# A written order for VectorE and ScalarE in the attention loop of a fused attention and mixture-of-experts kernel

## The chip, the cores and the metric

The kernel runs on one core of one Trainium2 chip. The time is device microseconds of one execution. Before the change it is 614.98 us, the median of three runs (613.36 to 615.66 us). The profile is that of one more execution, which took 612.03 us; what the profiler recorded of it spans 610.3 us.

The engines are named as in the profile: PE is the matrix engine (PEld its weight loads), DVE the vector engine, ACT the scalar engine, POOL the general engine, SP the engine that issues most transfers. A program holds one list of instructions for each engine; which of two instructions that could both run stands first in such a list is decided when the program is built, and that is the subject of this change.

## What is computed

The reference is sliding-window attention with sinks (4 batches, 8 heads, 768 positions, head size 64, window 128, the first 4 positions kept for everyone), and behind it a mixture of 8 experts in which a token may stay with the expert of the token before it:

```python
scores = scale * q @ k.T                      # per batch and head
keep = is_sink | ((rel >= 0) & (rel < window))
a = softmax(where(keep, scores, -1e9))
x = (a @ v)                                   # -> (B, S, 512)
logits = x @ w_gate;  local = sigmoid(x @ w_local)
for s in range(S):                            # per batch, in order
    e = argmax(logits[s]) if s == 0 or local[s] < 0.5 else e_of(s - 1)
    out[s] = softmax(logits[s])[e] * (relu(x[s] @ w1[e]) @ w2[e])
```

The choice of an expert needs the whole row of attention outputs of a token (all 8 heads), and it runs through the positions of a batch in order.

## The kernel before

**Attention.** The work is cut into 8 groups (`gi` 0 to 7: 4 batches times 2 halves of 4 heads), each into 6 blocks of 128 queries (`i` 0 to 5), each into two units of 2 heads (`c` 0 and 1; `k = 2 i + c` numbers the units of a group). A block sees its own 128 keys, the 128 before them and 8 sink columns, so a row of scores has 264 columns (128 in block 0, 256 in block 1). Float32 products are made exact enough by splitting queries and keys into a high and a low part: the high part is a cast by DVE or ACT (line 124), the low part a subtraction by POOL or DVE (line 129).

The loop (line 738) is a software pipeline over blocks. One turn of it, called here **the turn of block n**, does:

- `score` for both units of block n: 12 matmuls (line 539), then for each of the 4 heads an eviction on DVE, which adds the mask and finds the row's bound (line 543), and an exponential on ACT (line 546);
- `slot`: what belongs to other groups: loads, the split of the next group's queries and keys in four steps (`head`, at the units that `HEADS` names), in the last group the split of the first expert weights (`first_split`);
- `turn` of block n-1, unit 0: 4 transposes into PSUM (line 561) and a copy out by ACT (line 563);
- `apply` of block n-2, unit 1: 8 matmuls with the values (line 596), one for the sinks (line 602), and `finish`, four DVE instructions (lines 511 to 517);
- `turn` of block n-1, unit 1: the same, and for the sinks a transpose of a small tile (line 568), matmuls that prepare columns of the next group's values in the same PSUM bank (line 493), a copy by ACT (line 573), a subtraction by DVE (line 577) and a copy by DVE (line 464); behind the last block of a group three more DVE instructions (lines 474 to 479, `sink_rows`);
- `apply` of block n-1, unit 0; and one `step` of the routing.

The transposes and the sink tile share two PSUM buffers (`ps_t`). Three tiles go through them in a turn, so the sink transpose (line 568) takes the buffer that ACT's first copy of the turn (line 563) has to empty.

**Routing** of a batch begins two turns behind its last block, in the turn of block 1 of groups 2, 4 and 6, and goes on by one part per turn (two per turn in the last group): two reductions; eight small DVE instructions; a transpose of flags with copies by ACT; a scan over 768 positions (line 285); a second scan (line 289) with a product on POOL, or on DVE for the last batches (line 292); in block 0 of the next group a matmul (line 297) and seven small DVE instructions; then the scatter of the rows (line 312). The last batch is routed in two pieces, the first of them in the last turns of attention.

**What sets the order.** PE follows the program text (`manual_schedule(engines={ET.PE})`, line 727). DVE, ACT, POOL and SP are put in order by a planner that goes by its own estimate of when inputs are ready; `issue_after` gives it single constraints (for example, a split of the next group not ahead of the unit's last eviction and exponential). Behind attention, in the expert part, all engines but POOL follow the text.

**The start.** `lead0` splits the first 256 columns of group 0, `rest0` the others; the first two of `lead0`'s four steps stand ahead of the loop, the other two behind the first unit's scores. `products` and `logits` prepare group 0's own value columns, `rest` its sink rows.

Of the kernel before, what the change touches and what calls it, by code (L numbers as in the profile page):

```python
# [68 lines left out]
def kernel(ctx, tc, qkd, vn, vtd, vs, w1, w2, nw, c_misc, c_ident, c_small,  # L69
# [345 lines left out]
    def attention(fast):  # L415
        sfx = "f" if fast else "g"
        with ExitStack() as st:
# [17 lines left out]
            def group_steps(b, g, res):  # L435
# [17 lines left out]
                def products(j):  # L453
                    if j in ((0, 2) if fast else (0,)):
                        t["m"], t["j"] = ps_m.tile([P, NBLK * HG + 2 * WIDE, NW], F32, tag=m_tag, name=f"vw{n}_{j}"), j
                    for pr in range(npr):
                        o = ((j - t["j"]) * npr + pr) * 2
                        nc.tensor.matmul(t["m"][:, o:o + 2 * WIDE, :], vt_t[:, pr, j * P:(j + 1) * P],
                                         wb[:, g * npr + pr:g * npr + pr + WIDE, :], start=True, stop=True)

# [66 lines left out]
            def score(u):  # L527
# [13 lines left out]
                for t in range(2):  # L541
                    sm = p3.tile([P, N2], F32, tag="sm", bufs=4, name=f"sm{n}_{t}")
                    u["dve"] = nc.vector.tensor_tensor_reduce(out=sm[:, :w], in0=sps[:, t, :w], in1=mk, scale=-0.125,  # L543
                                                   scalar=BIG, op0=ALU.add, op1=ALU.min,
                                                   accum_out=bias[:, t:t + 1])
                    u["act"] = nc.scalar.activation(pe[:, t, :w], sm[:, :w], AF.Exp, bias=bias[:, t:t + 1], scale=-1.0)  # L546

                if c == 1 and i >= 2:
                    u["blk"]["pk"] = pk = p2.tile([P, 3, HG, SK], F32, tag="pk", name=f"pk{n}")
                    nc.vector.tensor_copy(  # L550
                        pk, u["blk"]["pe"][:, :, P:P + SK].unsqueeze(1).broadcast_to([P, 3, HG, SK]))

            def turn(u):
# [5 lines left out]
                for t in range(2):  # L559
                    for k, (j, o) in enumerate(tiles):  # L560
                        u["after"] = [nc.tensor.transpose(tp[:, t, k, :], pe[:, t, o:o + P], ident)]  # L561
                u["pt"] = pt = p3.tile([P, 2, 2, P], F32, tag="pt", name=f"pt{n}")
                u["after"].append(nc.scalar.copy(pt[:, :, 0:nt, :], tp[:, :, 0:nt, :]))  # L563
                if c == 1 and i >= 2:
                    nr, r0, r1 = 3 * HG * SK, HG * SK, 2 * HG * SK
                    both = ps_t.tile([P, 512], F32, tag="t", name=f"tps{n}")
                    tps = both[0:nr, 0:P]
                    nc.tensor.transpose(tps, u["blk"]["pk"].rearrange("p a h s -> p (a h s)"), ident)
                    if u["ahead"]:
                        vw = both[:, P:P + 2 * (HG + WIDE - 1) * NW].rearrange("p (x c) -> p x c", c=NW)  # L570
                        mm, out = u["ahead"]["spare"](vw, i)
                    u["blk"]["pts"] = pts = p2.tile([nr, P], F32R, tag="pts", name=f"pts{n}")
                    hi = nc.scalar.copy(pts, tps)
                    if u["ahead"]:
                        tc.add_manual_dep(hi.ins, mm.ins.name, mybir.DependencyInfo(
                            mybir.DependencyClass.Sync, mybir.DependencyReason.DATA), reason="one bank")
                    lo = nc.vector.tensor_tensor(out=pts[r0:r1], in0=tps[r0:r1], in1=pts.bitcast(F32)[r0:r1],  # L577
                                                 op=ALU.subtract)
                    u["after"].append(lo)
                    if u["ahead"]:  # L580
                        with tc.issue_after(lo.ins):
                            out()
# [83 lines left out]
            if fast:  # L666
# [12 lines left out]
                def slot(u, gi, k):  # L679
# [8 lines left out]
                    if gi == 0:  # L688
                        with tc.issue_after(units[k]["dve"].ins), tc.issue_after(units[k]["act"].ins):
                            for f in rest0[2 * k - 2:2 * k] if 0 < k < 3 else []:  # L690
                                f()
                        if k == RK:
                            with tc.issue_after(units[RK]["dve"].ins):
                                gst[0]["rest"]()
                        for x in LOADS.get(k, ()):
                            qk_load(x) if x > 1 else gst[nx]["load"][x]()
                        if k < 3:
                            gst[0]["products"](2 * k)
                            gst[0]["products"](2 * k + 1)
                        if k == 0:  # L700
                            gst[0]["logits"](0, 2)
# [25 lines left out]
                order.enter_context(tc.manual_schedule(engines={ET.PE}))  # L727

                def drain(u):
                    with ExitStack() as late:  # L730
                        for x in u["after"]:
# [543 lines left out]
```

## Time and profile before

| | |
|---|---|
| median of 3 runs | 614.98 us |
| profiled execution | 612.03 us |
| its span | 610.3 us |
| attention, until PE starts on the experts | 252.6 us |
| expert part | 357.7 us |
| PE busy in the span | 554.3 us (91%) |
| DVE, ACT, POOL busy | 373.5, 276.1, 209.9 us |

A row of the timeline has the start in us, the length in us, the engine, the line, the operation, output and inputs, the number of equal instructions merged in it, and in brackets how long the engine stood idle before it and what ended that. A row of the view by stretches has the stretch, its length, and for each engine the busy time and, in brackets, the number of instructions; then the clock granted to PE (1.00 is full), the share of the DMA engines and their rate. A row of the waits has the engine and line that waited, the engine and line that ended the wait, the us in total, the times, and the longest.

### The profile page before, as it was taken

How to read it: one execution, taken by the hardware profiler on the slowest of the kernel's cores; microseconds unless marked ns; L12 is line 12 of the kernel's file. 1: busy time of each engine (PE TensorE's matmuls, PEld its weight loads, DVE VectorE, ACT ScalarE, POOL GpSimd, SP SyncE). 2: the span in 40 equal slices, each digit the busy share in tenths (PEclk: the TensorE clock that was granted, in tenths of full speed). 3: DMA queues.
4: the chain of work that ended last, by engine and by line, in shares of the span. 5: the costliest groups of instructions: out<-in, count | busy, mean ns of one | idle time of the engine just before them, and what ended most of it. 6: DMA issues, size and time to landing. Idle time of an engine off the chain costs nothing. (4 is left out here: it accounts for less than half of the span.)

```text
span 610.3 us, 11598 instructions
## 1 busy us (share of the span) xinstructions
PE 554.3 (91%) x3872; PEld 485.6 (80%) x3872; DVE 373.5 (61%) x1268; ACT 276.1 (45%) x666; POOL 209.9 (34%) x147
## 2 busy tenths in 40 slices
PE   6799989998998879779789999989899799999995
PEld 4688978897997778667769978887887769888894
DVE  4667688778868988474637527464365767372421
ACT  2566675757566646232316218161532536132220
POOL 3233143714552750131516206253340355302201
PEclk8999999999999989789579999999999999999998
DMA  8645424643643232128438026484642629211000
GB/s 309 242 173 176 132 106 137 212 171 98 200 148 127 103 126 84 59 75 307 145 96 301 37 74 258 132 279 127 225 157 63 248 80 338 80 38 38 35 21 34
DMA packets 31481, 88.38 MB, mean 145 GB/s; under 512 B 3886, under 2 KB 5422, under 8 KB 31280
## 3 DMA queue, kind: packets, MB, share of 16 engines
q1 hardware_dynamic: 26528, 73.29, 35.8%
q0 software_dynamic: 4176, 12.64, 5.6%
q14 instruction: 147, 1.20, 0.7%
q8 instruction: 54, 0.88, 0.6%
q10 hardware_dynamic: 576, 0.36, 0.2%
HBM read 71.27 MB, written 16.06 MB: 143 GB/s over the span
## 5 line engine op out<-in xcount | busy, mean ns | idle before, releaser
L546 ACT ACTIVATE pef<-smf,biasf 128x264 f32<-128x264 f32 (+2 forms) x192 | 85.2, 488 | 79.2 <-DVE biasf L543 67.5
L596 PE MATMUL avf<-v,ptf 128*128 128x128 f32 (+1 forms) x704 | 96.9, 279 | 2.6 <-ACT ptf L563 2.2
L596 PEld LDWEIGHTS avf<-v,ptf 128*128 128x128 f32 x704 | 87.0, 193 | 5.4 <-ACT ptf L563 5.4
L543 DVE CUSTOM_DVE_ANT_0 smf<-sf,mask 128x264 f32<-128x264 f32 (+2 forms) x192 | 68.4, 403 | 16.1 <-PE sf L539 14.9
L978 ACT ACTIVATE hx<-h 128x256 fp32r<-128x256 f32 (+3 forms) x72 | 24.2, 360 | 109.2 <-PE h L967 94.4
L1016 PE MATMUL late<-w_a,hx 128*128 128x512 f32 (+2 forms) x288 | 68.8, 393 | 1.0 <-issue 1.0
L946 DVE SCALAR_TENSOR_TENSOR hx<-h,hx 128x256 fp32r<-128x256 f32 (+3 forms) x72 | 26.6, 390 | 67.7 <-ACT hx L978 66.1
L1016 PEld LDWEIGHTS late<-w_a,hx 128*128 128x128 f32 (+2 forms) x288 | 50.7, 179 | 14.4 <-issue 1.4
L1016 PE MATMUL late<-w_b,hx 128*128 128x512 f32 (+1 forms) x216 | 55.5, 414 | 2.8 <-SPq L891 2.3
L129 POOL TENSOR_TENSOR qk_b<-raw,qk_b 128x800 fp32r<-128x800 f32 (+1 forms) x16 | 31.1, 1942 | 77.1 <-PE avf L596 31.0
L561 PE MATMUL tpf<-ident,pef 128*128 128x128 f32 x352 | 56.9, 280 | 0.3 <-DVE ptsf L577 0.2
L998 POOL DMA_INDIRECT out_dram<-ot_d,oi_d x18 | 18.7, 1041 | 99.9 <-DVE ot_d L997 80.6
L1016 PEld LDWEIGHTS late<-w_b,hx 128*128 128x128 f32 (+1 forms) x216 | 41.9, 197 | 13.9 <-issue 2.5
L563 ACT COPY ptf<-tpf 128x512 f32<-128x512 f32 (+1 forms) x96 | 51.3, 535 | 3.4 <-PE tpf L561 3.1
L978 ACT ACTIVATE hx<-hs 128x96 fp32r<-128x96 f32 (+2 forms) x72 | 16.7, 273 | 70.7 <-DVE hs L961 63.7
L561 PEld LDWEIGHTS tpf<-ident,pef 128*128 128x128 f32 x352 | 39.4, 141 | 6.9 <-DVE ptsf L577 0.3
L847 POOL TENSOR_TENSOR w_b<-raw,w_b 128x1024 fp32r<-128x1024 f32 x10 | 25.6, 2558 | 39.7 <-ACT w_b L846 38.0
L847 POOL TENSOR_TENSOR w_c<-raw,w_c 128x1024 fp32r<-128x1024 f32 x11 | 27.3, 2486 | 33.5 <-ACT w_c L846 22.2
L847 POOL TENSOR_TENSOR w_a<-raw,w_a 128x1024 fp32r<-128x1024 f32 x10 | 26.5, 2649 | 30.1 <-ACT w_a L846 27.0
L967 PEld LDWEIGHTS h<-x_a,w_c 128*128 128x128 f32 x288 | 33.9, 188 | 1.7 <-issue 1.6
L129 POOL TENSOR_TENSOR w_a<-raw,w_a 128x800 fp32r<-128x800 f32 (+3 forms) x16 | 26.5, 1665 | 24.7 <-PE avf L596 13.3
L967 PE MATMUL h<-x_a,w_c 128*128 128x256 f32 x288 | 34.3, 279 | 0.8 <-DMA out_dram<-ot_d,oi_d 0.5
(239 smaller groups left out, 1063.7 us busy)
## 6 DMA issues: line engine op xcount, KB each, us to landing
raw<-in_dram SPq DMA_DIRECT2D x53, 512.0 KB, 6.1
raw<-in_dram SPq DMA_DIRECT2D x14, 800.0 KB, 4.4
vt<-in_dram SPq DMA_DIRECT2D x8, 864.0 KB, 4.7
v<-in_dram SPq DMA_DIRECT2D x7, 888.0 KB, 4.9
xr_0n<-xs SPq DMA_DIRECT2D x21, 258.0 KB, 4.1
raw_w<-in_dram SPq DMA_DIRECT2D x7, 512.0 KB, 5.8
raw<-in_dram SPq DMA_DIRECT2D x10, 256.0 KB, 3.0
xs<-zrun SPq DMA_DIRECT2D x9, 258.0 KB, 5.4
```

What stands on the lines that cost most here:

```text
L129: lows[e] = getattr(nc, e).tensor_tensor(out=out, in0=raw, in1=hi.bitcast(F32), op=ALU.subtract)
L543: u["dve"] = nc.vector.tensor_tensor_reduce(out=sm[:, :w], in0=sps[:, t, :w], in1=mk, scale=-0.125, scalar=BIG, op0=ALU.add, op1=ALU.min, ...
L546: u["act"] = nc.scalar.activation(pe[:, t, :w], sm[:, :w], AF.Exp, bias=bias[:, t:t + 1], scale=-1.0)
L561: u["after"] = [nc.tensor.transpose(tp[:, t, k, :], pe[:, t, o:o + P], ident)]
L563: u["after"].append(nc.scalar.copy(pt[:, :, 0:nt, :], tp[:, :, 0:nt, :]))
L596: nc.tensor.matmul(av[:, h, 0:w], u["pt"][:, t, k, :], u["prep"]["vf"][:, vo:vo + w], start=h == 0 and k == 0, stop=h == HG - 1 and k == l ...
L847: todo += [lambda s=s: lo(out=l[:, s], in0=raw[:, s], in1=h.bitcast(F32)[:, s], op=ALU.subtract) for s in ([slice(0, FF)] if eng[1] == "po ...
L946: nc.vector.scalar_tensor_tensor(out=d[:, :, 1, :], in0=h, scalar=0.0, in1=d.bitcast(F32)[:, :, 0, :], op0=ALU.max, op1=ALU.subtract)
L967: nc.tensor.matmul(hs, w[:, k, fs], x, start=t == 0, stop=t == len(mm) - 1)
L978: relu = nc.scalar.activation(d[:, :, 0, :], h, AF.Relu)
L998: s_i = nc.gpsimd.indirect_dma_start(out=out, out_offset=bass.IndirectOffsetOnAxis(ap=oi[0:m].bitcast(U32), axis=0), in_=ot[0:m], in_offse ...
L1016: nc.tensor.matmul(o, a, w, start=t == 0, stop=t == len(mm) - 1, skip_group_check=half)
```

## The change

DVE and ACT follow the program text in the attention loop, as PE does, and the text is rearranged for it. In a turn DVE now has: the four evictions; `finish`; the spread of the sink columns (line 550 before); the subtraction and copies behind the sink transpose; the DVE parts of `slot`; the DVE parts of the routing `step`. ACT has: the exponentials of unit 0; the copy of the first transposes; the exponentials of unit 1; the copy of the second transposes; the sink copy; the ACT parts of `slot`; those of the `step`. POOL and SP are still ordered by the planner.

Besides: the steps of the split move (`HEADS`), from units 4, 6, 8, 9 to 0, 4, 6, 8 in groups 1 to 6, and from 6, 7, 9, 10 to 4, 5, 7, 9 in group 0. All of `lead0` stands ahead of the loop, and all of `rest0` is in the turn of block 0, with one low part moved from DVE to POOL (`SENG2`). Group 0's products stand between the scores of its first two units, its `sink_mm` ahead of the copy out of the same bank. In the drain behind the last block, the transposes of the first experts' rows (`x_steps`) stand among the last turns, and the routing parts are no longer all in front of the last transposes.

```diff
-HEADS = (6, 7, 9, 10), (4, 6, 8, 9)
+HEADS = (4, 5, 7, 9), (0, 4, 6, 8)
+SENG2 = ("vector", "gpsimd", "act", "vector"), ("vector", "gpsimd", "act", "gpsimd")
...
-    rest0 = qk_split(0, SENG, False, slice(lead, S), slice(lead, KPAD))[0]
+    rest0 = qk_split(0, SENG2, False, slice(lead, S), slice(lead, KPAD))[0]
...
-        for f in lead0[0:2]:
+        for f in lead0:
...
                 def rest():
-                    logits(2, NBLK)
                     m2 = t["m"][0:nr, NBLK * HG, :]
                     sink_mm(m2)
+                    logits(2, NBLK)
                     sink_rows(m2)
...
-                    u["act"] = nc.scalar.activation(pe[:, t, :w], sm[:, :w], AF.Exp, bias=bias[:, t:t + 1], scale=-1.0)
...
+                def evict():
+                    for t in range(2):
...
+                def exps():
+                    for t in range(2):
...
+                def spread():
+                    if i >= 2:
...
+                return evict, exps, spread
...
+            def turn_sinks(u):
...
+                def rests():
+                    nc.vector.tensor_tensor(out=pts[r0:r1], in0=tps[r0:r1], in1=pts.bitcast(F32)[r0:r1],
+                                            op=ALU.subtract)
                     if u["ahead"]:
...
+                        out()
+
+                return rests
...
-                            for f in rest0[2 * k - 2:2 * k] if 0 < k < 3 else []:
-                                f()
+                        for f in rest0[2 * k:2 * k + 2]:
+                            f()
...
-                        with tc.issue_after(u["dve"].ins), tc.issue_after(u["act"].ins):
-                            head(nx, when.index(k))
+                        head(nx, when.index(k))
...
-                order.enter_context(tc.manual_schedule(engines={ET.PE}))
+                order.enter_context(tc.manual_schedule(engines={ET.PE, ET.DVE, ET.Activation}))
...
-                        score(u)
-                        for f in lead0[2:] if n + u["c"] == 0 else []:
-                            f()
-                    for u in now:
-                        slot(u, u["gi"], u["k"])
+                        parts.append(score(u))
+                        if n + u["c"] == 0:
+                            vw01 = [gst[0]["products"](j) for j in range(4)][0]
+                    for evict, _, _ in parts:
+                        evict()
+                    if now:
+                        parts[0][1]()
                     if a[0]:
                         turn(a[0])
+                    if now:
+                        parts[1][1]()
+                    if n == nu:
+                        xs_steps = [x_steps(xr0[j], early_x, j, f"{sfx}e{j}", ps_s, "s") for j in range(NE)]
                     if n >= 2 * NPR:
+                        if n > nu:
+                            while pend:
+                                step()
                         apply(z[1])
                         done(z[1]["b"], z[1]["g"], z[1]["i"])
+                    rests = None
                     if n == nu:
-                        drain(z[1])
+                        xs_steps[0][0]()
                     if a[1]:
                         turn(a[1])
+                        rests = turn_sinks(a[1])
+                    if n == nu:
+                        xs_steps[1][0]()
+                    if now:
+                        parts[1][2]()
+                    if rests:
+                        rests()
+                    if a[1]:
                         apply(a[0])
+                    if n == nu:
+                        for j in range(NE):
+                            xs_steps[j][1]()
+                    for u in now:
+                        slot(u, u["gi"], u["k"], vw01)
                     for _ in range(1 if n < nu - ST2 else 2):
-                        with tc.issue_after(now[-1]["dve"].ins) if now else ExitStack():
-                            step()
+                        step()
```

More of the change, by code (lines that the diff above doesn't have):

```diff
@@ L459, in products @@
                                          wb[:, g * npr + pr:g * npr + pr + WIDE, :], start=True, stop=True)
+                    return t["m"]
                 def logits(j0, j1, m=None):
@@ L560, in turn @@
                     for k, (j, o) in enumerate(tiles):
-                        u["after"] = [nc.tensor.transpose(tp[:, t, k, :], pe[:, t, o:o + P], ident)]
+                        nc.tensor.transpose(tp[:, t, k, :], pe[:, t, o:o + P], ident)
                 u["pt"] = pt = p3.tile([P, 2, 2, P], F32, tag="pt", name=f"pt{n}")
[L563 to L568, printed above, removed]
-                    if u["ahead"]:
[L570 to L582, printed above, removed]
@@ new lines, in turn @@
+                nc.scalar.copy(pt[:, :, 0:nt, :], tp[:, :, 0:nt, :])
+            def turn_sinks(u):
+                b, g, i, c = u["b"], u["g"], u["i"], u["c"]
+                n = f"{sfx}{b}_{g}_{i}_{c}"
+                if i < 2:
+                    return lambda: None
+                nr, r0, r1 = 3 * HG * SK, HG * SK, 2 * HG * SK
+                both = ps_t.tile([P, 512], F32, tag="t", name=f"tps{n}")
+                tps = both[0:nr, 0:P]
+                nc.tensor.transpose(tps, u["blk"]["pk"].rearrange("p a h s -> p (a h s)"), ident)
+                if u["ahead"]:
+                    vw = both[:, P:P + 2 * (HG + WIDE - 1) * NW].rearrange("p (x c) -> p x c", c=NW)
+                    mm, out = u["ahead"]["spare"](vw, i)
+                u["blk"]["pts"] = pts = p2.tile([nr, P], F32R, tag="pts", name=f"pts{n}")
+                hi = nc.scalar.copy(pts, tps)
+                if u["ahead"]:
+                    tc.add_manual_dep(hi.ins, mm.ins.name, mybir.DependencyInfo(
+                        mybir.DependencyClass.Sync, mybir.DependencyReason.DATA), reason="one bank")
+                def rests():
+                    nc.vector.tensor_tensor(out=pts[r0:r1], in0=tps[r0:r1], in1=pts.bitcast(F32)[r0:r1],
+                                            op=ALU.subtract)
+                    if u["ahead"]:
+                        out()
+                return rests
@@ L677, in head, with slot @@
                     preps[gi]["steps"][h]()
-                def slot(u, gi, k):
+                def slot(u, gi, k, vw01=None):
                     nx = gi + 1
@@ L726, in attention @@
                 order = ExitStack()
-                order.enter_context(tc.manual_schedule(engines={ET.PE}))
-                def drain(u):
-                    with ExitStack() as late:
-                        for x in u["after"]:
-                            late.enter_context(tc.issue_after(x.ins))
-                        while pend:
-                            step()
-                        for _ in early_prep(sfx, ps_s, "s"):
-                            pass
+                order.enter_context(tc.manual_schedule(engines={ET.PE, ET.DVE, ET.Activation}))
                 for n in range(0, nu + 2 * NPR, NPR):
-                    now = units[n:n + NPR]
+                    now, parts = units[n:n + NPR], []
+                    a, z = units[n - NPR:n] if 0 < n <= nu else [None, None], units[n - 2 * NPR:n - NPR]
                     for u in now:
@@ L743, in attention @@
                         if u["gi"] == 0 and u["k"] == 6:
-                            with tc.issue_after(units[5]["act"].ins), tc.issue_after(lows["gpsimd"].ins):
+                            with tc.issue_after(lows["gpsimd"].ins):
                                 xb_meta(0)
```

35 lines of the change are left out of this document (16 added, 19 removed).

## The prediction

> **What bounds the kernel now.** I read the view by stretches first, cut at the first score matmul of a group, then PE's waits. A routing group (the first row, group 2), a plain one (group 3), the last group, and from its last block to the experts:
>
> ```profile
> 67.67:96.99 29.32, 26.57 (x247) 23.84 (x246) 24.51 (x101) 19.36 (x45) 8.69 (x5) 1.00 0.36 124
> 96.99:123.89 26.90, 26.15 (x247) 24.18 (x246) 19.76 (x99) 17.63 (x42) 14.78 (x13) 1.00 0.60 192
> 210.10:236.41 26.31, 22.04 (x189) 19.92 (x189) 21.62 (x95) 14.06 (x37) 13.81 (x11) 0.94 0.35 123
> 236.41:252.62 16.21, 10.28 (x89) 9.26 (x88) 11.13 (x49) 6.29 (x16) 2.88 (x3) 0.97 0.15 53
> ...
> PE tpsf L568 <- ACT ptf L563: 10.4, 12, 1.8
> PE avf L602 <- DVE ptsf L577: 2.7, 1, 2.7
> PE avf L596 <- ACT ptf L563: 2.2, 6, 1.0
> PE tmf L297 <- DVE orr L292: 2.1, 1, 2.1
> ```
>
> PE sets the pace: in the plain group it idles 26.90 - 26.15 = 0.75 us, in a routing group 2.75, in the last 4.3. What it waits for is mostly ACT's first copy of a turn (10.4 us in 12 waits of the sink transpose). So the change can gain a few us at most in each group; where DVE or ACT come later than now, it loses.
>
> A turn without a stall, that of block 5 of group 1:
>
> ```profile
> 62.78 1.01 PE L539 MATMUL sf<-qk_b 64*128 64x264 f32 x12
> 63.49 0.43 DVE L543 CUSTOM_DVE_ANT_0 smf<-sf,mask 128x264 f32<-128x264 f32 x1 [0.22 <-PE sf L539]
> 64.02 0.92 ACT L546 ACTIVATE pef<-smf,biasf 128x264 f32<-128x264 f32 x2 [1.33 <-DVE biasf L543]
> 64.85 0.56 ACT L563 COPY ptf<-tpf 128x512 f32<-128x512 f32 x1
> 65.68 0.27 PE L568 MATMUL tpsf<-ident,pkf 128*96 128x128 f32 x1
> 66.88 0.26 ACT L573 CAST ptsf<-tpsf 96x128 fp32r<-96x128 f32 x1 [0.17 <-PE tpsf L493]
> 67.49 0.23 DVE L464 COPY v<-tpsf 128x72 f32<-128x72 f32 x1
> 67.67 0.89 PE L539 MATMUL sf<-w_a 64*128 64x128 f32 x12
> ```
>
> Here ACT already has the order that the change writes down: two exponentials, copy, two exponentials, copy. Let e be how far into a turn the first eviction starts; here 63.49 - 62.78 = 0.71. The copy starts 1.36 behind it and ends at 65.41, 0.27 ahead of the sink transpose (2.90 into the turn). DVE's last copy ends at 67.72, 0.05 into the next turn, and the next eviction could start 0.71 into it. **So 0.66 us of DVE work fit behind the copies; what is longer makes the next e late.**
>
> **The routing turns** show what a late e costs:
>
> ```profile
> 134.30 1.89 POOL L129 TENSOR_TENSOR qk_b<-raw,qk_b 128x800 fp32r<-128x800 f32 x1 [14.12 <-PE avf L596]
> 134.90 1.32 DVE L264 SCALAR_TENSOR_TENSOR frf<-lgf,small 128x6 f32<-128x6 f32 x1
> ...
> 140.15 0.31 PE L568 MATMUL tpsf<-ident,pkf 128*96 128x128 f32 x1 [1.77 <-ACT ptf L563]
> ...
> 144.75 3.00 DVE L285 TENSOR_TENSOR_SCAN orr<-kpf,fof 8x768 fp32r<-8x768 bf16 x1
> ...
> 149.22 0.43 DVE L543 CUSTOM_DVE_ANT_0 smf<-sf,mask 128x264 f32<-128x264 f32 x1
> 150.64 1.80 DVE L289 TENSOR_TENSOR_SCAN ctf<-ones,zrun,orr 8x768 f32<-8x768 f32 x1
> 151.20 0.31 PE L568 MATMUL tpsf<-ident,pkf 128*96 128x128 f32 x1 [0.74 <-ACT ptf L563]
> ...
> 237.06 0.15 DVE L264 SCALAR_TENSOR_TENSOR frf<-lgf,small 128x3 f32<-128x3 f32 x1
> ```
>
> The planner put the scan behind the evictions, and the next first eviction came late (149.22); the sink transpose followed it by 151.20 - 149.22 = 1.98. So **PE's stall is e + 1.98 - 2.90 = e - 0.92**. And line 264 took 1.32 beside POOL's low part, ending at 136.22 with it (136.19), against 0.15 alone: POOL holds such instructions up until it is done.
>
> **The change, part by part.** Unstalled turns (blocks 3 to 5 of plain groups) stay: the cast fits the 0.66, ACT's cast of queries lies behind its sink copy, long before the next exponential. A queries step also issues a load on SP; it moves at most two turns forward, its data are wanted a group later: nothing.
>
> *Key cast in block 0* (groups 1, 2, 4, 6). It stands behind the sink rows and ahead of the evictions of block 1:
>
> ```profile
> 184.82 0.98 PE L539 MATMUL sf<-w_a 64*128 64x256 f32 x12
> 185.34 0.46 DVE L479 TENSOR_TENSOR srf<-sxf,srf 32x296 fp32r<-32x296 f32 x1
> 185.83 0.42 DVE L543 CUSTOM_DVE_ANT_0 smf<-sf,mask 128x256 f32<-128x256 f32 x1
> 187.57 0.71 PE L596 MATMUL avf<-v,ptf 128*128 128x128 f32 x4 [0.15 <-ACT ptf L563]
> 189.82 0.57 DVE L124 CAST qk_b<-raw 128x800 fp32r<-128x800 f32 x1
> ```
>
> The sink rows end 0.98 into the turn, e is 1.01 and PE already waits 0.15 (stall e - 0.86). The cast adds its 0.57 in full: 4 x 0.57 = +2.3. Behind it on DVE are the evictions, for them ACT waits, for ACT PE. A gain is excluded: DVE has no gap there.
>
> *Stalls of plain groups.* Casts between evictions or ahead of a copy go:
>
> ```profile
> 112.53 0.31 PE L568 MATMUL tpsf<-ident,pkf 128*96 128x128 f32 x1 [0.47 <-ACT ptf L563]
> 131.97 0.97 DVE L247 TENSOR_REDUCE lgf<-lw 128x54 f32<-128x432 f32 x1
> 217.03 1.07 DVE L303 TENSOR_SCALAR smf<-smf 128x6 f32<-128x6 f32 x1
> ```
>
> 0.47 here, and some 0.15 of line 596's 2.2 us in 6 waits: -0.6 in groups 1, 3, 5, -1.8 (0 to -2.3, the whole 0.75 of idling).
>
> *Routing groups 2, 4, 6.* Now 1.77 + 0.74 and a small one, 2.7 of the 2.75. In the new order each part stands at the end of DVE's list, straight ahead of the evictions. Block 2: `finish` ends with the turn before it, the reduction (0.97, with its second 1.2) comes behind, e = 1.2, stall 0.4 by block 1's rule. Block 3: eight small instructions, 0.15 to 0.2 each, 1.3 in all, e = 1.4, stall 0.5. Block 4: ACT's copies of the flags ahead of its exponentials, 0.4 as an estimate from 0 to the 0.74. Block 5: the scan, 1.80 like the second one if unheld (3.00 beside POOL): e = 0.05 + 0.1 + 1.8 = 2.0, stall 1.1. Sum 2.4, so -0.3 each, **-0.9**; if POOL holds block 3's instructions for a low part (1.89), +1.7 each, +4.2.
>
> *Blocks 0 and 1 of groups 3 and 5.* Block 0: the second scan (1.80) gives e = 1.9; its evictions are half as long, so I take 0.8. Block 1: behind the sink rows (0.6 into the turn, PE being late too) come the cast (0.57) and the seven small instructions behind line 297's matmuls (1.2): e = 2.4, stall 1.6. But the cast starts POOL's low part, 1.89 long, and line 303 was held beside POOL work (1.07): then e = 0.6 + 0.57 + 1.9 + 0.9 = 4.0, stall 3.1. The held rows are the nearest, so 0.8 + 3.1 = 3.9 twice: **+7.8** (unheld +4.8).
>
> *Start.*
>
> ```profile
> 15.68 1.19 PE L539 MATMUL sf<-w_a 64*128 64x256 f32 x12
> 16.55 0.42 DVE L543 CUSTOM_DVE_ANT_0 smf<-sf,mask 128x256 f32<-128x256 f32 x1 [1.50 <-PE sf L539]
> 19.92 0.51 PE L468 MATMUL vwf<-misc,vt 128*96 128x9 f32 x4 [1.97 <-DVE v L464]
> 21.80 1.00 PE L539 MATMUL sf<-w_a 64*128 64x264 f32 x12
> ```
>
> Sink matmuls ahead of the copy remove 1.97. PE's first turn ends earlier, but DVE now has all of `rest0` in front of block 1's evictions, which stay at about 16.6. Taken -1.5 (0, if `rest0` comes later still, to -3.4, the 1.97 with 1.4 of the earlier scores).
>
> *Last group.*
>
> ```profile
> 217.56 0.45 PE L568 MATMUL tpsf<-ident,pkf 128*96 128x128 f32 x1 [1.30 <-ACT ptf L563]
> 219.21 1.96 PE L596 MATMUL avf<-v,ptf 128*128 128x128 f32 x8
> 224.78 1.00 PE L539 MATMUL sf<-qk_b 64*128 64x264 f32 x12
> 249.92 0.18 DVE L517 TENSOR_TENSOR lw<-avf,rsf 128x36 f32<-128x36 f32 x1
> ```
>
> In blocks 0 and 1 PE lost 2.7 (line 602), 1.30, and about 1.7 by matmuls at twice their length (8 in 1.96): 5.7. Weight splits no longer stand among these scans. New: scan and product, 2.8 in all, e = 2.9, stall 1.7; then 15 small instructions, e = 3.0, stall 2.1: 3.8, so -1.9 (-3.9 to 0). Tail, 236.41 to 250.10: the wait for line 297 (2.1) stays, since its two scans still run in the last turns, now with only the last `apply` behind it; transposes of the experts' rows fill about 1 of it, while splits and two routing parts make block 5's evictions about 2 late: +1.0 (-2.1 to +4).
>
> Sum: 2.3 - 1.8 - 0.9 + 7.8 - 1.5 - 1.9 + 1.0 = **+5.0**. The profiled execution took 612.03 us, so 617.0; the median of the runs is 614.98, 2.95 above it, so 620.0 for a median.
>
> The clock: line 596's 8 matmuls took 1.96 at 219.21, behind two gaps of 2.67 and 1.30. The Trainium skill (TensorE: Matmul & The Clock Gate, The HAM clock gate) wants an idle window of some 3.4 us before the clock halves; by that page stalls of 3.1 cost no clock, and the sum stays. The row shows the slowing with work between the gaps, so it speaks for the second rival below; no run here yet shows a gap of 3.1.
>
> **The rivals.**
> 1. *The wanted gain.* DVE catches up inside the turn: the casts and routing parts, ready at once, run while PE is in `apply`, so the terms for the key cast and for groups 3 and 5 are nil. For: DVE is busy only 24.51 of 29.32 us. Against: its order is one list, and the parts stand where 0.66 is free. It decides for the gain if evictions in routing turns start below e = 0.92. Then -1.8 - 0.9 - 1.5 - 1.9 + 1.0 = -5.1: 609.9.
> 2. *Clock and holds on top.* Each stall of 3.1, and the tail's, halves the clock for as long as 219 shows (1.7): three times 1.7 = +5.1, 625.1; with holds in block 3 (+1.7 three times) 630.
> 3. *Stalls only change place.* POOL starts later, nothing is held (-3.0), and the start gains 3.4 (-1.9): +0.1, 615.1. That the planner's order was already the written one speaks for it in plain turns only.
>
> **Chances.** Forecast 0.42 (own range 617 to 623), rival 1 0.22, rival 2 0.16, rival 3 0.20. No change means within 0.5%, 3.1 us. Slower: 0.42 + 0.16 = 0.58; same 0.20; faster 0.22. The range 609 to 626 leaves out the lower half of rival 1 and the holds of rival 2, some 0.18.
>
> **What would show it.** First evictions of block 1 in groups 3 and 5 at e near 4 with line 596 waiting about 3; in groups 2, 4, 6 at 1.6 with 0.7; line 568 waiting in blocks 2 to 5 for 0.4 to 1.1 instead of 1.77; line 468 no longer waiting at 20 us. Line 596 waiting under 1 in groups 3 and 5 would make the prediction wrong.

## The result: 617.11 us after 613.81 us, and the profile after

The changed kernel took 617.11 us (median; 613.58 to 623.62), the kernel before 613.81 us beside it (609.63 to 618.86): the ratio is 1.0057, with a 95% interval of 1.0033 to 1.008. It is slower, by about 3.3 us.

The profiled execution of the changed kernel took 620.67 us, 3.6 above its own median, that of the kernel before 612.03, 1.8 below its. The traces therefore differ by 8.6 us where the medians differ by 3.3. The changed kernel was profiled a second time on another chip (run *after_again* below: 616.14 us beside 614.13, a difference that is not clear of the noise); what both profiles show is the change, what only one shows is that execution.

The view by stretches of the changed kernel, cut at the first score matmul of a group as in the prediction (columns: from:to, length, busy time of PE, weight loads, DVE, ACT and POOL, granted clock, DMA share, GB/s):

```profile
68.15:96.99 28.84, 26.62 (x247) 23.84 (x247) 22.17 (x101) 19.43 (x45) 8.82 (x4) 1.00 0.34 115
96.99:126.42 29.43, 26.41 (x247) 24.20 (x246) 22.03 (x99) 17.60 (x42) 15.81 (x13) 1.00 0.52 184
...
213.55:238.62 25.07, 21.72 (x189) 19.83 (x189) 18.97 (x89) 13.98 (x35) 10.91 (x10) 0.93 0.38 136
238.62:259.28 20.66, 12.86 (x89) 11.69 (x88) 15.60 (x52) 7.61 (x19) 5.64 (x5) 0.79 0.10 33
```

The same view of the second execution, group 3 and the last stretch:

```profile
95.53:126.08 30.55, 27.78 (x248) 25.53 (x248) 22.13 (x99) 17.70 (x42) 15.46 (x13) 0.94 0.51 177
...
238.27:258.04 19.77, 11.93 (x88) 10.90 (x88) 15.58 (x52) 7.50 (x19) 5.46 (x5) 0.88 0.10 31
```

| stretch (us) | before | after | again | after - before | predicted |
|---|---|---|---|---|---|
| start, to block 2 of group 0 | 21.80 | 22.17 | 20.61 | +0.37 / -1.19 | -1.5 |
| rest of group 0 | 19.25 | 19.55 | 19.67 | +0.30 | 0 |
| group 1 (plain) | 26.62 | 26.43 | 26.44 | -0.19 | 0 |
| group 2 (routing; 4 is alike) | 29.32 | 28.84 | 28.81 | -0.48 | +0.3 |
| group 3 (plain) | 26.90 | 29.43 | 30.55 | +2.53 / +3.65 | +3.3 |
| group 5 (plain) | 26.90 | 29.43 | 29.42 | +2.53 | +3.3 |
| group 6 (routing) | 29.97 | 28.79 | 28.82 | -1.18 | +0.3 |
| group 7, blocks 0 to 4 | 26.31 | 25.07 | 25.05 | -1.24 | -1.9 |
| last block to the experts | 16.21 | 20.66 | 19.77 | +4.45 / +3.56 | +1.0 |
| experts | 357.68 | 359.12 | 356.96 | +1.44 / -0.72 | 0 |

Groups 3 and 5 and the last stretch lose; groups 1, 2, 4, 6 and 7 gain a little; the start and the experts differ in sign between the two executions. PE's waits of the changed kernel between 20 and 262 us (total, times, longest), against the 10.4, 2.7, 2.2 and 2.1 us that the prediction shows:

```profile
PE avf L615 <- ACT ptf L575: 11.8, 14, 2.1
PE tpsf L585 <- ACT ptf L575: 9.7, 11, 3.1
PE tmf L298 <- DVE orr L293: 2.7, 1, 2.7
```

PE still waits for ACT's copy of transposes, but now it is `apply` (line 615) as much as the sink transpose (line 585). Block 1 of group 3, in order of time, shows the chain:

```profile
103.53 0.58 DVE L125 CAST w_a<-raw 128x800 fp32r<-128x800 f32 x1
104.32 0.17 DVE L304 TENSOR_SCALAR smf<-smf 128x6 f32<-128x6 f32 x1
104.34 1.89 POOL L130 TENSOR_TENSOR w_a<-raw,w_a 128x800 fp32r<-128x800 f32 x1 [3.50 <-DVE smf L303]
105.07 1.19 DVE L310 TENSOR_TENSOR xb<-ppf,smf 128x6 f32<-128x6 f32 x1
106.18 0.41 DVE L548 CUSTOM_DVE_ANT_0 smf<-sf,mask 128x256 f32<-128x256 f32 x1
106.69 0.91 ACT L554 ACTIVATE pef<-smf,biasf 128x256 f32<-128x256 f32 x2 [4.79 <-DVE biasf L548]
107.50 0.35 ACT L575 COPY ptf<-tpf 128x256 f32<-128x256 f32 x1
107.91 0.71 PE L615 MATMUL avf<-v,ptf 128*128 128x128 f32 x4 [2.12 <-ACT ptf L575]
```

The key cast and seven routing instructions stand ahead of the evictions; the last of them (line 310) is held until POOL's low part is done, at 106.23. ACT has been idle for 4.79 us: its next two instructions are exponentials, and the copy that `apply` needs stands behind them. The last group's block 5 has the same chain, and there PE waits 3.13 us:

```profile
240.36 0.47 DVE L257 TENSOR_TENSOR eqf<-lgf,mxf 128x24 f32<-128x24 f32 x1
240.87 1.20 DVE L258 TENSOR_TENSOR eqf<-eqf,small 128x24 f32<-128x24 f32 x1
242.83 0.43 DVE L548 CUSTOM_DVE_ANT_0 smf<-sf,mask 128x264 f32<-128x264 f32 x1
...
244.81 0.45 PE L585 MATMUL tpsf<-ident,pkf 128*96 128x128 f32 x1 [3.13 <-ACT ptf L575]
245.05 1.92 PE L615 MATMUL avf<-v,ptf 128*128 128x128 f32 x8
```

The last row is the clock: eight matmuls in 1.92 us at a granted clock of 0.5, where the same eight took 1.06 us one turn earlier (the stretch has 0.79 on the mean). The rows by stretches divide the loss of this stretch. PE is busy for 12.86 us where it was 10.28, and idle for 7.80 where it was 5.93; in the second execution it is 11.93 and 7.84. So 1.9 us of the loss are idle time in both, and 2.6 or 1.7 us are the same matmuls at half clock.

### The profile page after: what moved, and what is told of

Its sections match the earlier page's. It is cut to its first block, busy times and chain, and to the rows that moved or that the text cites. A ratio compares the mean times of both kernels' runs of the same rounds, so it can differ in the third digit from the quotient of the medians.

```text
span 618.4 us, 11603 instructions
## 1 busy us (share of the span) xinstructions
PE 556.9 (90%) x3872; PEld 489.1 (79%) x3872; DVE 370.2 (60%) x1267; ACT 276.1 (45%) x666; POOL 211.1 (34%) x148
## 5 line engine op out<-in xcount | busy, mean ns | idle before, releaser
L615 PE MATMUL avf<-v,ptf 128*128 128x128 f32 (+1 forms) x704 | 99.5, 284 | 11.8 <-ACT ptf L575 11.8
L615 PEld LDWEIGHTS avf<-v,ptf 128*128 128x128 f32 x704 | 89.5, 198 | 15.1 <-ACT ptf L575 15.1
L548 DVE CUSTOM_DVE_ANT_0 smf<-sf,mask 128x264 f32<-128x264 f32 (+2 forms) x192 | 66.6, 401 | 14.4 <-PE sf L541 13.8
L573 PE MATMUL tpf<-ident,pef 128*128 128x128 f32 x352 | 58.7, 287 | 4.1 <-DMA xs<-zrun 3.5
L130 POOL TENSOR_TENSOR qk_b<-raw,qk_b 128x800 fp32r<-128x800 f32 (+1 forms) x16 | 33.8, 2116 | 74.4 <-ACT qk_b L125 27.6
L130 POOL TENSOR_TENSOR w_a<-raw,w_a 128x800 fp32r<-128x800 f32 (+4 forms) x17 | 28.2, 1659 | 35.3 <-ACT w_a L125 9.5
```

Of the source, the lines that this page charges most:

```text
L130: lows[e] = getattr(nc, e).tensor_tensor(out=out, in0=raw, in1=hi.bitcast(F32), op=ALU.subtract)
L548: u["dve"] = nc.vector.tensor_tensor_reduce(out=sms[t][:, :w], in0=sps[:, t, :w], in1=mk, scale=-0.125, scalar=BIG, op0=ALU.add, op1=ALU.m ...
L615: nc.tensor.matmul(av[:, h, 0:w], u["pt"][:, t, k, :], u["prep"]["vf"][:, vo:vo + w], start=h == 0 and k == 0, stop=h == HG - 1 and k == l ...
```

## The experiments

Three theories stood at the start. **T** is the prediction's: DVE work that stands straight ahead of the evictions sets the time. **U**: the loop is neutral, the loss is in the last group and the tail. **V**: the clock adds to each long stall. The runs were made on three chips: *heads_old*, *heads_mid*, *step_mid* and *fsk2* on one, where the kernel before took 625.25 us; *after_again*, *pe_only*, *pe_act* and *step_fin* on a second (614.13); the last four on a third (625.13). Ratios are each to the kernel before on the same chip.

**The splits back in the old blocks** (*heads_old*).

```diff
-HEADS = (4, 5, 7, 9), (0, 4, 6, 8)
+HEADS = (6, 7, 9, 10), (4, 6, 8, 9)
```

> The fixed order stays, only the splits go back to the blocks of the kernel before (key casts at the end of blocks 2 and 4 in groups 1 to 6, none in block 0). Theory T (DVE work that stands straight ahead of the evictions sets the time): the 0.58 us cast leaves the way to block 1, so the stalls of 0.63 to 0.64 us in block 1 of groups 1, 2, 4 and 6 fall to 0.1 (-2.2 us), the 2.12 us ones of groups 3 and 5 fall to 0.5 (-3.2 us), and blocks 3 and 5 get 0.2 to 0.6 us each back where a cast and a routing part now share a turn's end (+2 us): about -3.5 us against the changed kernel, ratio to the kernel before 1.000. Theory U (the loop is neutral, the loss is in the last group and the tail): within 0.5 us of the changed kernel, ratio 1.006.

Measured: 638.77 us, ratio 1.0215 [1.0175, 1.0255]: far slower than the changed kernel, where T expected a gain. T's first half holds: block 1 of groups 1, 2, 4 and 6 stalls 0.15 us, of groups 3 and 5 0.75. The price of its second half, +2 us, was far too low, for two reasons, shown by group 2 (POOL and DVE, then the waits, then stretches of 3.4 us):

```profile
82.81 1.89 POOL L130 TENSOR_TENSOR qk_b<-raw,qk_b 128x800 fp32r<-128x800 f32 x1 [13.50 <-issue]
82.83 1.94 DVE L258 TENSOR_TENSOR eqf<-eqf,small 128x48 f32<-128x48 f32 x1
96.41 3.37 DVE L286 TENSOR_TENSOR_SCAN orr<-kpf,fof 8x768 fp32r<-8x768 bf16 x1
...
87.47 0.31 PE L585 MATMUL tpsf<-ident,pkf 128*96 128x128 f32 x1 [2.33 <-ACT ptf L575]
101.65 0.32 PE L585 MATMUL tpsf<-ident,pkf 128*96 128x128 f32 x1 [2.75 <-ACT ptf L575]
...
85.10:88.50 3.40, 1.06 (x10) 1.03 (x10) 2.86 (x16) 2.47 (x6) 0.00 (x0) 1.00 0.00 0
88.50:92.00 3.50, 3.50 (x25) 2.85 (x24) 1.41 (x7) 2.74 (x7) 1.82 (x1) 0.51 0.00 0
...
98.80:102.20 3.40, 0.65 (x6) 0.56 (x6) 3.14 (x13) 2.00 (x5) 2.64 (x1) 1.00 0.00 0
102.20:105.60 3.40, 3.40 (x20) 3.18 (x21) 2.12 (x4) 0.94 (x3) 0.00 (x0) 0.50 0.70 242
```

A cast and a routing part that share a turn's end start a low part on POOL, which holds one DVE instruction until it is done (line 258, 1.94 instead of 0.20) or stretches the scan (3.37). And each stall of over 2 us leaves PE busy for 1.06 or 0.65 of 3.4 us; in the next 3.4 us the granted clock is 0.5, with PE busy throughout: about 1.7 us more for each. With a fixed order, then, the new blocks of the splits are a needed part of the change; the key cast in block 0 is their price.

**The splits inside the turn** (*heads_mid*): in groups 1 to 6 `head(...)` is called behind the second pair of exponentials, ahead of `apply(z[1])`, instead of in `slot`.

```diff
...
+                    for u in now:
+                        if u["gi"]:
+                            heads_of(u["gi"], u["k"])
                     if n >= 2 * NPR:
```

(`heads_of` is a new function; it holds the lines of `slot` that call `head`.)

> One move: in groups 1 to 6 the splits of the next group (cast on DVE, copy on ACT, low parts on POOL) are written behind the second pair of exponentials and ahead of the turn's apply, in the same blocks as in the changed kernel. Theory T: the cast of 0.58 us no longer stands ahead of block 1's evictions: stalls of 0.64 us in groups 1, 2, 4, 6 fall to 0.1 (-2.2 us), and in groups 3 and 5 2.12 us fall to 1.5 or less, the POOL hold going to an earlier instruction (-1.2 to -3): -4 us against the changed kernel, ratio 0.999. Theory U: no change, ratio 1.006.

Measured: 630.04 us, ratio 1.0065 [1.0041, 1.009]. The stalls named did shrink (0.64 to 0.15, 2.12 to 1.28), but blocks 3 and 5 of the routing groups now wait 1.69 and 1.79 us: the cast is ahead of `finish` and the sink subtraction instead. PE's waits at line 585 sum to 19.3 us, against 9.7: what the move gained was given back two blocks on. The total is that of U and not of T; the waits show that this is two effects that cancel, and not a neutral loop.

**The routing parts inside the turn** (*step_mid*), at the same place:

```diff
+                    if now:
+                        for _ in range(1 if n < nu - ST2 else 2):
+                            step()
                     if n >= 2 * NPR:
...
-                    for _ in range(1 if n < nu - ST2 else 2):
-                        step()
+                    if not now:
+                        step()
+                        step()
```

> One move: the routing part of a turn is written behind the second pair of exponentials and ahead of the turn's apply, so in DVE's list it stands between the evictions and finish instead of ahead of the next evictions. Theory T: block 1 of groups 3 and 5 stalls under 0.5 us where it stalled 2.12 us, and their block 0 nothing (-4.9 us), the stalls of 1.6 us that groups 2, 4 and 6 each have in blocks 2 to 5 shrink to 0.4 (-3.6 us), the 3.13 us wait ahead of the last block's sink transpose to 1 us (-2 us); finish and the sink subtraction come 1 to 2 us later and may give 2 us back: -7 us (-4 to -10) against the changed kernel, ratio 0.994. Theory U: only the wait in the tail moves, -2 us, ratio 1.002. If the parts merely change place (the stall goes to the apply behind a late finish), ratio 1.006 as the changed kernel.

Measured: 622.8 us, ratio 0.9963 [0.9931, 0.9994]; direction as T says. The size is open, since the changed kernel was not run on this chip: against its 1.0057 or 1.0022 on two others it is 5.9 or 3.7 us, where T named 7 (4 to 10). Block 1 of groups 3 and 5 no longer stalls. A wait of 3.07 us came into their block 3 (see the last section), and new ones of 0.41 and 1.66 appear in block 4 of the routing groups, behind ACT's copies of the flags, which now stand ahead of its copy of transposes:

```profile
90.61 0.77 ACT L277 COPY fof<-tff 8x768 bf16<-8x768 bf16 x1
91.40 0.79 ACT L279 COPY kpf<-tff 8x768 bf16<-8x768 bf16 x1
92.10 0.24 ACT L283 ACTIVATE exf<-exf 128x48 f32<-128x48 f32 x1
92.36 0.58 ACT L575 COPY ptf<-tpf 128x512 f32<-128x512 f32 x1
```

**The routing parts behind `finish`** (*step_fin*), as *step_mid* but behind `apply(z[1])` and `done(...)`.

```diff
                         done(z[1]["b"], z[1]["g"], z[1]["i"])
+                    if now:
+                        for _ in range(1 if n < nu - ST2 else 2):
+                            step()
                     rests = None
```

> The routing part of a turn is written behind finish and ahead of the second block of transposes, so that neither the evictions nor finish wait for it; the sink subtraction and the copy of the second transposes do. Theory T: the stalls of 2 to 3 us that the earlier place of the part put into blocks 3 and 4 shrink under 1.5 us, since finish comes 1 to 2.5 us earlier, and block 1 of groups 3 and 5 stalls under 0.7 us: ratio 0.991 (0.987 to 0.996). If the copies on ACT and the matmuls on PE behind the part's results are what waits, its blocks 3 and 4 stall 2 us or more again and the ratio is 0.996 to 1.002.

Measured: 613.15 us, ratio 0.9975 [0.9945, 1.0005], beside 1.0022 for the changed kernel on the same chip. Groups 3 and 5 take 28.3 us instead of 30.6 and 29.4, the routing groups 29.2 instead of 28.8; the wait for line 279 stays, at 5.0 us in 4 waits. The ratio is that of the second case of the expectation; the stalls, at most 1.5 us each, are smaller than it named.

**The splits of the experts' first weights one block earlier** (*fsk2*).

```diff
-FSK, ST2 = 4, 12
+FSK, ST2 = 2, 12
```

> One number: the eight splits of the experts' first weights start in block 1 of the last group and not in block 2, so none is left for block 5 and only two for block 4. Theory U (the tail holds the loss): the held routing instructions of 0.47, 1.20 and 1.25 us in blocks 4 and 5 take under 0.3 us each, the wait ahead of the last sink transpose falls from 3.13 to 1.2 us, the stretch from block 5 to the experts from 20.7 to 17 us: -3.5 us, ratio 1.000. Theory T: the tail gains the same, but blocks 1 to 3 of the last group lose 0.4 to 0.7 us each to the casts: -2 us, ratio 1.002. If the stretch is long by the halved clock and not by the holds, it stays above 19.5 us and the ratio at 1.005.

Measured: 623.76 us, ratio 0.997 [0.994, 0.9999]. The hold of line 258 is gone (0.18 us), that of line 257 is not (0.47), and a cast, a low part of 0.68 on DVE and a routing part still stand ahead of block 5's evictions: the wait fell only from 3.13 to 2.55, and a wait of 2.33 came into block 2. By its profile the last group takes 48.3 us (28.92 + 19.39) where the changed kernel's took 45.7; where the gain against the kernel before comes from, the profile doesn't say, and the changed kernel wasn't run on this chip. U isn't borne out, and not refuted by this run.

**The changed kernel again** (*after_again*, no edit).

> The changed kernel once more, unchanged, beside the next three kernels on one chip. If its loss is a property of its order, 1.0057 again (1.003 to 1.009). Theory V (a stall of about 2 us is doubled when it falls whole into one 3.41 us window of the clock, and where it falls is chance) expects another set of halved windows in this profile: those of the tail again, and perhaps block 1 of groups 3 and 5, whose 2.12 us stalls straddled a window's edge in the first profile; such a group then takes 31.6 to 32.2 us instead of 29.4.

Measured: 616.14 us, ratio 1.0022 [0.9995, 1.0049], below the range that was expected: on this chip the loss is not clear of the noise. The stalls repeat to some 0.02 us, 2.13 and 2.12 in block 1 of groups 3 and 5 among them. What the clock makes of them doesn't repeat: of these four stalls in the two profiles one was followed by a half clock. First the changed kernel's first profile (group 3), then this one (groups 3 and 5):

```profile
103.90:107.30 3.40, 1.89 (x17) 1.51 (x14) 3.26 (x15) 0.61 (x2) 2.64 (x2) 1.00 0.68 240
107.30:110.70 3.40, 2.79 (x27) 2.52 (x28) 2.45 (x13) 2.48 (x8) 2.49 (x4) 1.00 0.94 377
```

```profile
103.10:106.50 3.40, 1.27 (x12) 1.04 (x10) 3.26 (x15) 1.26 (x4) 2.84 (x2) 1.00 0.73 254
106.50:109.90 3.40, 3.40 (x19) 2.94 (x20) 1.61 (x9) 1.57 (x5) 2.72 (x3) 0.50 0.90 353
...
164.50:167.90 3.40, 2.00 (x20) 1.75 (x21) 2.47 (x15) 2.32 (x7) 2.76 (x3) 1.00 0.91 296
167.90:171.30 3.40, 3.15 (x31) 2.65 (x29) 2.22 (x12) 3.32 (x7) 2.49 (x4) 1.00 0.92 358
```

A stall that lies whole in one window (PE busy 1.27 of 3.40) is followed by a halved one; one that straddles the edge (1.89, 2.00) is not. That is V in kind; the group with the halved window took 30.55 us, less than the 31.6 to 32.2 that V named. How much of the spread of one kernel's executions (613.58 to 623.62 us) the clock makes isn't shown: of the 20, the one with 621.07 has a mean granted clock of 0.954, and so has the one with 614.58.

**Which engine's list costs?** The order fixed on PE alone, as before, with all of the new text (*pe_only*):

```diff
-                order.enter_context(tc.manual_schedule(engines={ET.PE, ET.DVE, ET.Activation}))
+                order.enter_context(tc.manual_schedule(engines={ET.PE}))
```

> The changed text, its splits and its arrangement, but the order is fixed on PE alone as in the kernel before; DVE's and ACT's lists are the planner's again. If the fixed order on DVE and ACT is what costs, the holds ahead of evictions go: ratio 0.998 (0.995 to 1.001). If the splits and the arrangement of the text cost, 1.005 (1.003 to 1.008) stays. If the fixed order is what still gives something, above 1.008.

Measured: 605.92 us, ratio 0.9868 [0.9833, 0.9902], further than any case of the expectation. So the rearranged text and its splits gain 8.2 us (605.92 - 614.13), and fixing DVE's and ACT's lists costs 10.2 (616.14 - 605.92, same chip). In group 3 (by stretches, then block 1 in order of time):

```profile
97.05:124.06 27.01, 26.28 (x248) 24.13 (x247) 20.40 (x98) 17.60 (x42) 15.03 (x13) 1.00 0.54 192
```

```profile
93.78 8.03 POOL L130 TENSOR_TENSOR w_a<-raw,w_a 128x768 fp32r<-128x768 f32 x4
103.46 0.41 DVE L548 CUSTOM_DVE_ANT_0 smf<-sf,mask 128x256 f32<-128x256 f32 x1
103.80 0.17 DVE L310 TENSOR_TENSOR xb<-ppf,smf 128x6 f32<-128x6 f32 x1
103.98 0.51 ACT L554 ACTIVATE pef<-smf,biasf 128x256 f32<-128x256 f32 x1 [2.71 <-DVE xb L310]
104.39 0.35 ACT L575 COPY ptf<-tpf 128x256 f32<-128x256 f32 x1
104.64 1.31 ACT L554 ACTIVATE pef<-smf,biasf 128x256 f32<-128x256 f32 x3
```

The planner does three things here that the written order forbids: all four low parts run in one stretch, 8.03 us from block 5 of the group before, clear of the routing parts (line 310 takes 0.17 now); routing instructions stand among the evictions; and the copy stands behind one exponential, the other three behind it. Block 1 doesn't stall.

**DVE's list free, ACT's fixed** (*pe_act*: `engines={ET.PE, ET.Activation}`).

> As the changed kernel, but DVE's list is the planner's again; PE's and ACT's orders stay fixed. Theory T (DVE's fixed list with casts and routing parts ahead of evictions costs): the stalls of 2.12 us in groups 3 and 5 fall under 1 us and the tail from 20.7 to 18 us or less, ratio 0.997 to 1.000, as with the order fixed on PE alone. If ACT's fixed list costs, it stays at 1.004 or more.

Measured: 615.01 us, ratio 1.0029 [1.0003, 1.0055]. The ratio falls between the two cases, and T isn't enough: the stalls of block 1 in groups 3 and 5 do go (the groups take 28.1 us), and still only 1.1 of the 10.2 us come back. The planner now puts weight splits and held routing instructions ahead of evictions in group 6's last block, and ACT, which can't take its copies past the exponentials, passes the delay on: there PE waits 1.51 us for DVE's sink subtraction and 1.62 for ACT's copy, and for that copy 2.63 in block 3 of group 0. PE's waits of this run, then of *pe_only*:

```profile
PE tpsf L585 <- ACT ptf L575: 11.4, 14, 2.6
PE avf L615 <- ACT ptf L575: 3.4, 12, 0.8
```

```profile
PE tpsf L585 <- ACT ptf L575: 8.7, 10, 2.0
PE avf L615 <- ACT ptf L575: 1.9, 8, 0.4
```

**ACT's list free, DVE's fixed** (*pe_dve*: `engines={ET.PE, ET.DVE}`). By now a theory S had been formed from *pe_only*: the splits that the fixed lists pin to their blocks are the cost.

> As the changed kernel, but ACT's list is the planner's again; PE's and DVE's orders stay fixed. Theory S (what the fixed lists cost is that they pin the splits of the next group to the blocks they are written in, where POOL's low parts hold routing instructions; with the order fixed on PE alone all eight parts ran in one stretch behind the last scores of a group): ACT's casts come free, DVE's key casts stay in blocks 0 and 3, so about half of the 10 to 11 us come back: ratio 0.997 (0.992 to 1.002). If ACT's fixed list alone costs: 0.987 to 0.990. If DVE's: 1.004.

Measured: 622.15 us, ratio 0.9954 [0.9924, 0.9983]. Inside S's range, but the next run decides against S. Beside that run (613.78 us, same chip, both lists free, splits pinned) DVE's fixed list alone costs 8.4 us. ACT's alone costs 9.1 (615.01 - 605.92) and both together 10.2: as far as two chips can be compared, the two costs don't add. That either list alone is enough to pass a late eviction on would explain it, and is not shown beyond that.

**The splits pinned, the rest free** (*pe_guard*: as *pe_only*, and)

```diff
-                        head(nx, when.index(k))
+                        with tc.issue_after(u["dve"].ins), tc.issue_after(u["act"].ins):
+                            head(nx, when.index(k))
```

> The order is fixed on PE alone, as in the run with 0.9868, but the splits of the next group may not be scheduled ahead of their own turn's last eviction and last exponential, as in the kernel before; their blocks stay 0, 2, 3 and 4. Theory S: most of the gain goes, the low parts on POOL stand in blocks 0 to 4 again: ratio 0.999 (0.995 to 1.003). If the gain of that run comes from the rest of DVE's and ACT's lists (routing instructions among the evictions, copies among exponentials): 0.985 to 0.990.

Measured: 613.78 us, ratio 0.9828 [0.9785, 0.987]: S falls. Pinning the splits alone costs nothing that can be seen (0.9868 without it, on another chip). The gain is in the rest of the two lists. The profile has many small waits (16.9 us for line 585 in 17 waits, none over 1.9), and from 20 to 256 us no halved clock.

**The other way round: the kernel before, splits free** (*before_free*).

```diff
-                        with tc.issue_after(u["dve"].ins), tc.issue_after(u["act"].ins):
-                            head(nx, when.index(k))
+                        head(nx, when.index(k))
```

> The kernel before with one thing undone: the splits of the next group no longer have to wait for their turn's last eviction and last exponential, in the same blocks of the text. Theory S: its loop gains as the changed text did with PE's order alone fixed, 1.5 to 2 us in each of groups 2, 4 and 6, and nothing in groups 3 and 5: -4 to -6 us, ratio 0.992 (0.989 to 0.996). If the rest of the new text is what gave those 8 us: 1.000 (0.996 to 1.003). If the product on POOL now stands behind three low parts, the last matmuls of a routing wait 4 us in groups 2, 4 and 6: 1.005 or more.

Measured: 624.99 us, ratio 1.0019 [0.9987, 1.005]. Second case: free splits in the old text and the old blocks gain nothing, so it is the rest of the new text, its new blocks included, that gave those 8 us.

**A version that beats both** (*pe_best*: as *pe_only*, and two holds). In *pe_only*, DVE stood still for 4.17 us in the last group, at a copy that the planner had put ahead of evictions:

```profile
229.18 0.17 DVE L356 COPY xm<-xr 128x2 int32<-128x2 int32 x1 [4.17 <-DMA xr<-xs]
```

```diff
-                        for f in rest0[2 * k:2 * k + 2]:
-                            f()
+                        with tc.issue_after(u["dve"].ins), tc.issue_after(u["act"].ins):
+                            for f in rest0[2 * k:2 * k + 2]:
+                                f()
...
-                        xs_steps[0][0]()
+                        with tc.issue_after(units[-1]["dve"].ins), tc.issue_after(units[-1]["act"].ins):
+                            xs_steps[0][0]()
```

and the same for `xs_steps[1][0]()`.

> The order fixed on PE alone, with two holds: the casts of the first group's rest not ahead of their unit's eviction and exponential, and the first tokens' transposes not ahead of the last unit's. In the run with 0.9868 the planner put a copy that waits 4.17 us for the rows' load in DVE's list ahead of the last two blocks' evictions (PE waited 2.10 and 2.03 us there, the next window of the clock was halved), and the scores waited 4.4 us in all for evictions of the first block. Both waits go: -2 us at the start, -4 to -6 us in the last group, ratio 0.978 (0.973 to 0.985). If they only change place (the load is awaited by the last transposes instead): 0.985 to 0.988.

Measured: 610.51 us beside 625.13, ratio 0.9765 [0.9733, 0.9798], the fastest against the kernel before. In the profile the wait in the last group is gone (24.89 + 13.68 us, *pe_only* 27.60 + 15.30), the start is not shorter (24.5 us to block 2, *pe_only* 23.7): the scores wait 4.42 us once where they waited 2.1 and 2.2. How much of the step from 0.9868 is the holds and how much the chip can't be told, since the two ran on different chips.

## Why the prediction was right, and where it wasn't

It said 620.0 with a range of 609 to 626 and slower as likeliest; 617.11 and 1.0057 came. Step by step:

- **The rule "stall = e - 0.92" held.** In block 5 of the last group the first eviction starts 242.83 - 238.62 = 4.21 into the turn; the rule gives 3.29, PE waited 3.13. In block 1 of group 3 it starts 106.18 - 102.88 = 3.30 in (4.0 predicted); e - 0.86, the prediction's rule for that block, gives 2.44, PE waited 2.12. It was read from the kernel before, whose ACT list had the same order in plain turns, and it carried over.
- **Key cast, +2.3: right.** Block 1 of groups 1, 2, 4 and 6 stalls 0.62 to 0.64 us in both profiles and 0.15 where the cast is moved away: 4 x 0.49 = 2.0.
- **Groups 3 and 5, +7.8: right in place and kind, too large.** Block 0 stalls 0.64 (predicted 0.8), block 1 2.12 (3.1 held, 1.6 unheld). The hold happened, but to one instruction only, the last: POOL's low part began at 104.34, when three of the seven had started, and the next three ran beside it unheld (0.17 to 0.20 us). Stall for stall that is 5.5 instead of 7.8; rival 3's "nothing is held" didn't come.
- **Routing groups, -0.9 in all: too cautious.** Stalls of blocks 2 to 5: 0.54, 0.11, 0.28 and 0.65, 1.6 us where 2.4 were predicted; the first scan cost least against its price (0.65, not 1.1), and nothing in block 3 was held.
- **Start, -1.5:** -1.19 in one execution, +0.37 in the other. The wait for the sink matmuls went, and PE waited 3.5 us at line 573 instead, for a buffer of transposes that the logits' copy (line 466), behind all of `rest0`, gives back; *fsk2*'s view names that copy, 3.5 us.
- **Last group, -1.9:** -1.24; stalls 1.62 and 1.73 for 1.7 and 2.1. The stalls were right, the gain two thirds of what was named.
- **Tail, +1.0: the term that was mis-sized, +4.45 and +3.56.** The prediction had block 5's evictions "about 2 late"; they were 4.21 into the turn, because two of block 4's routing instructions were held (0.47 + 1.20 us, rows above). The hold that the prediction priced for block 3 struck here, where it had taken none. The idle part of the loss is 1.9 us in both executions. Beside it stand 2.6 and 1.7 us of halved clock, behind that stall and behind the wait for line 298 (2.68 us); the sum had put the clock at nothing.
- **The clock.** Rival 2 was right in kind: stalls well under 3.4 us do halve the clock, but by chance of position, not always. The Trainium skill (TensorE: Matmul & The Clock Gate, The HAM clock gate) states a free-running window, and the runs agree with that: the window's edges stay and the stalls move against them. Its rule that an idle window of about 3.4 us comes first does not hold here: a stall of 2.13 us inside one window was enough.
- **What would have made it wrong**, a wait of under 1 us for line 615 in groups 3 and 5, didn't come.

What the prediction lacked is the split of the sum. It took the change for a small sum of stalls around an order that was there already. By the runs it is two large terms of opposite sign: the rearranged text is worth -8.2 us under the planner's lists, and writing DVE's and ACT's lists down costs +10.2. The sum of the stalls could still come out near, since it was priced in the one version in which both are present. That it came so near is in part luck: by the table the last stretch lost 3.5 us (2.6 in the second execution) and the start 1.9 (0.3) more than predicted, while the three routing groups together lost 3.0 less. The prediction put the stalls to DVE's list alone; *pe_act* shows that with DVE free and ACT fixed only 1.1 us come back: a late eviction costs PE time through ACT's list, and that has to be free as well.

**Open.** Which part of the new text gives the 8.2 us under PE's fixed order wasn't tried; it isn't the freedom of the splits (*pe_guard*, *before_free*). Which of the planner's two liberties, routing among evictions or the copy behind one exponential, counts for how much is argued from one block's rows and not shown.

## What to carry over

Fix an order on the engine that sets the pace and on no other without a run that leaves the others to the planner: a written list on an engine with slack takes away what that slack was good for. A stall is better split: the many waits of *pe_guard*, up to 1.9 us long, halved no clock, while one of 2 to 3 us can cost up to 1.7 more than its length. And where work must stand ahead of evictions, keep what starts POOL's elementwise work out of the same turn.

## What was not expected of the hardware

- The clock is decided in windows of 3.4 us by how busy PE was in the last one: busy for 0.65, 1.06 and 1.27 us it was halved for the next, for 1.89 and 2.00 it was not (rows above). All 14 profiles of this case agree: each change of the granted clock, always between 1.00 and 0.50, lies on one grid of 3.41 us in its trace. Between 20 and 256 us they have 910 such windows at full clock. Where PE was busy for under 1.5 us, the next one was halved in all 29 cases; for over 2.1 us, in none of 835; in between, in 13 of 46.
- Two of the chips are slower for the kernel before, 625.25 and 625.13 us against 614.13, with the same mean granted clock of 0.95. On both, in block 3 of groups 3 and 5 (in *pe_best* of group 3 alone), around the end of the six scatters of rows on POOL, the first eviction comes late though its scores are there. The same turn on the slower chip (*fsk2*) and on the faster one (*after_again*):

```profile
113.88 0.43 DVE L548 CUSTOM_DVE_ANT_0 smf<-sf,mask 128x264 f32<-128x264 f32 x1 [1.88 <-PE tpf L573]
```

```profile
112.68 0.43 DVE L548 CUSTOM_DVE_ANT_0 smf<-sf,mask 128x264 f32<-128x264 f32 x1 [0.72 <-PE sf L541]
```

The scores began at 112.04 and 112.00. In *before_free*, the nearest to the kernel before that was profiled on such a chip, it starts 3.55 and 3.35 us into the turn, in the kernel before, on a faster one, 0.68 and 0.71. Whether this makes up the 11 us isn't shown. The cause stays open; it is a reason to compare ratios on one chip only.
